# Reordering the products of an expert layer, moving the combinations of one slot, and moving two PSUM copies from ScalarE to VectorE

## Chip, cores and metric

The kernel runs on one core of one Trainium2 chip. The metric is the time of one execution in microseconds (us), measured on the device. A profiled execution gives a span that is about 1.7 us shorter than that time; spans are compared with spans, and times with times.

## The reference

The reference is an attention over 4 batches, 8 heads, 768 positions and head size 64 (causal; in five of the heads only sinks and a window are kept), followed by 8 experts over 3,072 tokens of width 512:

```python
out = 0
for e in range(8):
    h = np.maximum(x @ w1[e], 0.0)      # 3072x512 @ 512x1024
    out += P[:, e:e+1] * (h @ w2[e])    # 1024x512; P from 8 rounds of row/column scaling
```

## The kernel before

The attention, the first expert without its weights P, and the rounds that give P run first (0 to 178 us). Then come experts 1 to 7 in chunks of 512 tokens: 42 pieces of work called works. While layer 1 of one work runs, layer 2 of the work before runs too. Both multiply by Strassen's scheme in Winograd's form: seven products in place of eight, at the price of sums before and after, made by VectorE and ScalarE.

Layer 1 of a work has two halves g of seven products. Three PSUM banks (y, z, w) collect them. Some banks are read in the middle of a sum: after product 1, ScalarE copies bank y, then TensorE adds product 6 into the same bank.

```python
def step(g, k):
    if k == 1: product(g, 1, "y", first=True);            copy(g, "1", "y")     # ScalarE
    if k == 2: product(g, 2, "z", first=True, last=True); relu_sum(g, 0, 0, "z", "1")  # VectorE
    if k == 6: product(g, 6, "y");                        copy(g, "2", "y")
    if k == 5: product(g, 5, "w", first=True);            copy(g, "5", "w")
    if k == 7: product(g, 7, "y");                        relu_sum(g, 1, 1, "y", "5")
    if k == 3: product(g, 3, "w", last=True);             relu_sum(g, 0, 1, "w", "2")
    if k == 4: product(g, 4, "y", last=True);             # last read of y: a ReLU on ScalarE

for pair in (((0, 1), (0, 2)), ((0, 6), (0, 5)), ((0, 7), (0, 3)), ((1, 1), (0, 4)),
             ((1, 6), (1, 5)), ((1, 7), (1, 2)), ((1, 3), (1, 4))):
    for g, k in pair:
        step(g, k)
    yield                      # one pair of products per slot
```

A copied sum goes into a buffer R1, R2 or R5. A work has seven slots, numbered from 0 as in the code. Each slot issues one pair of layer 1's products, then perhaps combinations (sums of weights "w" or of inputs "x", on VectorE), then one product of layer 2, then perhaps a scaling of the first expert's sums ("first", on ScalarE) or a combination of h:

```python
for slot in range(7):
    go("l1", 2 if n == 0 and slot == 0 else 1)
    if slot in (1, 3):
        go("w")
        go("x", 2)             # only while e == 1
    go("l2")
    if slot in (2, 3, 5, 6):
        go("first")            # weight_first: acc = acc * Pne, 4 a work, only while e == 1
    if slot in (2, 3):
        go("h")
# ... the whole loop under
with tc.manual_schedule(engines={mybir.EngineType.DVE}):
```

The last line matters: in the expert stage only VectorE (DVE) runs in the order of the program. For TensorE and ScalarE the compiler's scheduler picks the order.

In attention the values of the first batch arrive in another layout and are put in place through PSUM, a third at a time:

```python
def place_v(g):
    for n in range(2):
        t = ...                # PSUM, two matmuls with an identity
        nc.scalar.activation(out=v_tile(0)[:, :, 2*g + n, 0:D], in_=t..., func=AF.Copy, bias=0.0, scale=1.0)
```

The softmax here doesn't subtract the row's maximum and nothing guards it: scores larger than these inputs give would overflow.

Of the kernel before, what the change touches and what calls it, by code (L numbers as in the profile page):

```python
# [13 lines left out]
AF = mybir.ActivationFunctionType  # L14
# [22 lines left out]
def kernel(  # L37
# [13 lines left out]
    nc = tc.nc  # L51
    B, H, S, D = q.shape
# [48 lines left out]
    def v_tile(b):  # L101
        if b not in vts:
            vts[b] = ap.tile([128, H, NC, DV], F16, tag="v16", name=f"v16_{b}")
            nc.vector.memset(vts[b][:, :, :, D:DV], 1.0)
        return vts[b]
# [11 lines left out]
    def place_v(g):  # L117

        for n in range(2):
            t = psA.tile([128, 512], F32, tag="mo", bufs=3, name=f"vp_{g}_{n}")  # L120
            rows = slice(64 * n, 64 * n + 64)
            for c in range(2):
                nc.tensor.matmul(
                    out=t[64 * c:64 * c + 64, :].rearrange("p (h d) -> p h d", h=H),
                    lhsT=ident16[rows, rows], rhs=vraw[g][rows, :, c, :], start=True, stop=True,
                )
            nc.scalar.activation(
                out=v_tile(0)[:, :, 2 * g + n, 0:D], in_=t.rearrange("p (h d) -> p h d", h=H),
                func=AF.Copy, bias=0.0, scale=1.0,
            )  # L130

    def load_v_heads(b, h0, h1):
        for o in range(2):
# [15 lines left out]
    def load_expert(e):  # L149
        return load_w1(e), load_w2(e)  # L150
# [15 lines left out]
    def round_first(h0):  # L166
# [9 lines left out]
        out=ret_u,  # L176
        in_=is_retrieval.bitcast(U32).unsqueeze(0).broadcast_to([128, 2 * H]),
# [209 lines left out]
    def run(g, n):  # L387
        for _ in range(n):
            if next(g, "end") == "end":
                return False  # L390
        return True

    units = [(b, g, u) for b in range(B) for g in range(3) for u in range(2)]
    with tc.manual_schedule(engines={mybir.EngineType.Pool}):
        nc.gpsimd.affine_select(
            out=ident16, in_=ident16, compare_op=ALU.is_equal, fill=0.0,
            base=0, pattern=[[-1, 128]], channel_multiplier=1,
        )
        for o in range(2):
# [3 lines left out]
                out=f4, in_=f4, compare_op=ALU.is_ge, fill=0.0,  # L403
# [4 lines left out]
                out=w4, in_=w4, compare_op=ALU.is_ge, fill=0.0,  # L408
# [118 lines left out]
    with tc.manual_schedule(engines=engines):  # L527
# [11 lines left out]
        emit_prep(*preps.pop())  # L539
        warm(2)  # L540
        place_v(0)
        soften(r0, (1,))
        sum_later(0)
# [9 lines left out]
        sum_later(1)  # L553
        r3 = scores(3)
        place_v(1)
        finish_sums(lambda: emit_prep(*preps.pop()))
        soften(r3, (0,))
# [46 lines left out]
    for it in range(8):  # L604
# [3 lines left out]
            out=Pne, in0=Pne, in1=rr.unsqueeze(2).broadcast_to([128, NB, E]), op=ALU.mult  # L608
        )
        nc.vector.tensor_reduce(  # L610
            out=bs, in_=Pne.transpose([0, 2, 1]), axis=AX.X, op=ALU.add
# [5 lines left out]
        if it == 7:  # L617
            nc.vector.tensor_scalar(
                out=rcs, in0=rcs, scalar1=float(NTOK) / E, scalar2=None, op0=ALU.mult
            )  # L620
        nc.vector.tensor_tensor(
            out=Pne, in0=Pne, in1=rcs.unsqueeze(1).broadcast_to([128, NB, E]), op=ALU.mult
# [14 lines left out]
    def weight_first(c):  # L637

        for nb in range(4 * c, 4 * c + 4):
            nc.scalar.activation(out=acc_of(nb), in_=acc_of(nb), func=AF.Copy,  # L640
                                 bias=0.0, scale=Pne[:, nb, 0:1])
            yield
# [23 lines left out]
    def combine_w(e):  # L666
        w1, w2 = expw[e]
        X = mp.tile([128, 4, 2, 512], F16, tag="S1", name=f"S1_{e}")
        yield from left(lefts1, e, [[w1[:, 2 * k:2 * k + 2, ts(i, 512)] for k in range(2)]
                                    for i in range(2)], [X[:, j] for j in range(4)])  # L670
        X = mp.tile([128, 4, 4, 256], F16, tag="T2", name=f"T2_{e}")
        yield from right(rights2, e, [[w2[:, 4 * k:4 * k + 4, ts(n, 256)] for n in range(2)]
                                      for k in range(2)], [X[:, j] for j in range(4)])

    def combine_x(c):
        X = mp.tile([128, 4, 2, 256], F16, tag=f"T1_{c}", bufs=1, name=f"T1_{c}")
        yield from right(rights1, c, [[xT[k][:, :, CH * c + 256 * n:CH * c + 256 * n + 256]
                                       for n in range(2)] for k in range(2)],
                         [X[:, j] for j in range(4)])

    def combine_h(e, c):
        h = hTs[e, c]
        X = [mp.tile([128, 2, 4, 128], F16, tag=f"S2{j}", bufs=1, name=f"S2{j}_{e}_{c}")
             for j in range(4)]
        yield from left(lefts2, (e, c), [[h[:, :, 4 * k:4 * k + 4, ts(i, 128)] for k in range(2)]
                                         for i in range(2)], X)

    def new_h(e, c):
        hTs[e, c] = mp.tile([128, 2, 8, 256], F16, tag="hT", name=f"hT_{e}_{c}")
# [16 lines left out]
    def layer1(e, c):  # L706

        new_h(e, c)
        h = hTs[e, c]
        banks, R = {}, {}  # L710

        def product(g, k, bank, first=False, last=False):
            if first:
                banks[g, bank] = psB.tile([128, 2, 256], F32, tag="l1", name=f"l1{bank}")
            for f in range(2):
                for dc in range(2):
                    nc.tensor.matmul(  # L717
                        out=banks[g, bank][:, f, :],
                        lhsT=lefts1[e][k - 1][:, dc, ts(2 * g + f, 128)],
                        rhs=rights1[c][k - 1][:, dc, :], start=(first and f == 0 and dc == 0),  # L720
                        stop=(last and f == 1 and dc == 1), skip_group_check=True,
                    )

        def copy(g, name, bank):
            R[name] = mp.tile([128, 2, 256], F32, tag=f"R{name}", bufs=1, name=f"R{name}")
            nc.scalar.activation(out=R[name], in_=banks[g, bank], func=AF.Copy, bias=0.0, scale=1.0)  # L726

        def block(g, i, n):
            return h[:, n, 4 * i + 2 * g:4 * i + 2 * g + 2, :]

        def relu_sum(g, i, n, bank, name):
            nc.vector._custom_dve(TENSOR_ADD_SAT, out=block(g, i, n), in0=banks[g, bank],
                                  in1=R[name], s0=65504.0, s1=0.0)

        def step(g, k):
            if k == 1:
                product(g, 1, "y", first=True)
                copy(g, "1", "y")
            if k == 2:
                product(g, 2, "z", first=True, last=True)  # L740
                relu_sum(g, 0, 0, "z", "1")
            if k == 6:
                product(g, 6, "y")
                copy(g, "2", "y")
            if k == 5:
                product(g, 5, "w", first=True)
                copy(g, "5", "w")
            if k == 7:
                product(g, 7, "y")
                relu_sum(g, 1, 1, "y", "5")  # L750
            if k == 3:
                product(g, 3, "w", last=True)
                relu_sum(g, 0, 1, "w", "2")
            if k == 4:
                product(g, 4, "y", last=True)
                nc.scalar.activation(out=block(g, 1, 0), in_=banks[g, "y"], func=AF.Relu,
                                     bias=0.0, scale=1.0)

        for pair in (((0, 1), (0, 2)), ((0, 6), (0, 5)), ((0, 7), (0, 3)), ((1, 1), (0, 4)),
                     ((1, 6), (1, 5)), ((1, 7), (1, 2)), ((1, 3), (1, 4))):  # L760
            for g, k in pair:
                step(g, k)
            yield
# [88 lines left out]
    def go(name, n=1):  # L852
        run(gens[name], n)

    def body(n):
        e, c = works[n]
        if c == 0 and e + 1 < E:
            expw[e + 1] = load_expert(e + 1)
        if c == 2 and e + 1 < E:
            gens["w"] = combine_w(e + 1)  # L860
        if e == 1:
            gens["first"] = weight_first(c)
            gens["x"] = combine_x((c + 1) % NCH)
        for slot in range(7):
            go("l1", 2 if n == 0 and slot == 0 else 1)
            if slot in (1, 3):
                go("w")
                go("x", 2)
            go("l2")
            if slot in (2, 3, 5, 6):  # L870
                go("first")
            if slot in (2, 3):
                go("h")
            if n == 0 and slot == 0:
                run(combine_w(1), 9)
        if n + 1 == len(works):
            gens["l2"] = layer2_last(e, c)
            return
        gens["h"] = combine_h(e, c)
        go("h", 2)  # L880
        gens["l2"] = layer2(e, c)
        gens["l1"] = layer1(*works[n + 1])

    with tc.manual_schedule(engines={mybir.EngineType.DVE}):
        for n in range(len(works)):
            body(n)
        go("l2", 9)
# [35 lines left out]
```

## Time and profile before

| | before |
|---|---|
| time, median of the first three runs | 702.01 us |
| span of the profiled run | 700.3 us |
| start to the third placement's matmuls | 31.79 us |
| from there to a fixed transpose behind the affected rounds (first matmul into tr_0_1) | 11.70 us |
| from there to the last step of the weights P | 134.16 us |
| from there to the last matmul (expert stage) | 518.25 us |
| waits of TensorE in the expert stage, above its normal spacing | 2.96 us |

The four stretches come from the start times of named matmuls in the trace. The last row adds, over the matmuls of the expert stage, what the distance between two starts exceeds 109 ns for 256 columns (216 ns for 512), where the excess is over 30 ns. The normal spacing is what the Trainium skill gives ("TensorE: Matmul & The Clock Gate", "Wait — 56ns, not 53.3ns?"): columns / 2.4 GHz + about 2.5 ns, which is an estimate of 109 ns for 256 columns; the trace agrees (median 109 ns). The wait that the profile prints in brackets is smaller than this excess, because it starts at the modelled end of the previous matmul. At 187.00 us, for instance, the list has 0.30 us and the spacing 0.46 us.

The table of stretches of the kernel before; each engine column is its busy time in 20 us, with the number of instructions (PE is TensorE, PEld its weight loads, DVE VectorE, ACT ScalarE, POOL GpSimd; PEclk is the granted TensorE clock as a share of full speed):

```profile
core 0: us, PE busy (x) PEld busy (x) DVE busy (x) ACT busy (x) POOL busy (x), PEclk, DMA share, GB/s
180.00:200.00 20.00, 19.02 (x149) 14.40 (x148) 16.22 (x33) 20.00 (x39) 1.80 (x2) 1.00 0.49 81
200.00:220.00 20.00, 19.52 (x176) 16.75 (x174) 19.32 (x40) 14.29 (x30) 3.38 (x4) 1.00 0.37 64
220.00:240.00 20.00, 19.97 (x184) 17.67 (x182) 19.28 (x39) 11.61 (x24) 5.07 (x6) 1.00 0.43 75
260.00:280.00 20.00, 20.00 (x186) 17.94 (x184) 16.76 (x32) 10.95 (x24) 5.14 (x6) 1.00 0.79 129
```

From 260 us on, TensorE has no gap. Between 180 and 240 us it executes fewer instructions, and ScalarE is first busy all the time, then VectorE nearly so. TensorE's waits in that stretch, from the list of waits of the kernel before (engine, line waited for <- releaser: total us, times, longest):

```profile
PE l1y L717 <- ACT R_3696 L726: 0.5, 1, 0.5
PE l1y L717 <- ACT R_3540 L726: 0.4, 1, 0.4
PE l1y L717 <- ACT R_3517 L726: 0.3, 1, 0.3
PE l1y L717 <- ACT R_3618 L726: 0.3, 1, 0.3
```

All four are products into bank y behind ScalarE's copy of that bank. The timeline of the kernel before shows why the copy is late (start us, us, engine, line, operation, out<-in, count, wait and releaser in brackets):

```profile
186.32 0.63 ACT L726 ACTIVATE R_3517<-l1y 128x512 f32<-128x512 f32 x1
186.80 1.98 ACT L640 ACTIVATE acc_80<-acc_80,Pne 128x512 f32<-128x512 f32 x3
187.00 0.60 PE L717 MATMUL l1y<-T_1_3466,S_1_3450 128*128 128x256 f16 x4 [0.30 <-ACT R_3517 L726]
...
188.63 0.63 ACT L726 ACTIVATE R_3540<-l1y 128x512 f32<-128x512 f32 x1
...
189.32 0.60 PE L717 MATMUL l1y<-T_1_3466,S_1_3450 128*128 128x256 f16 x4 [0.41 <-ACT R_3540 L726]
```

Product 6 starts at 187.00. Where ScalarE is free, such a copy starts about 0.7 us after its product does (in a later work, 410.30 after 409.62). Here R_3540 begins only at 188.63, 1.63 us after the product, because three scalings (L640) stand before it in ScalarE's order.

The small waits of 0.19 us look like this in the timeline of the kernel before (VectorE's lines and TensorE's, in order of time):

```profile
215.23 0.42 DVE L663 TENSOR_TENSOR T_4_3911<-xT_76 128x512 f16<-128x512 f16 x1
...
216.03 0.87 DVE L798 SCALAR_TENSOR_TENSOR acc_81<-l2w,Pne,acc_81 128x256 f32<-128x256 f32 x2
...
216.81 0.68 DVE L732 CUSTOM_DVE_ANT_0 hT_3_3872<-l1y,R_3908 128x512 f16<-128x512 f32 x1
...
216.92 0.60 PE L717 MATMUL l1y<-xT_76,w_1_2386 128*128 128x256 f16 x4
...
217.54 0.60 PE L717 MATMUL l1y<-T_3_3730,w_1_2386 128*128 128x256 f16 x4
```

The relu sum of product 7 (L732, out of bank y) ends at 217.49. Product 4, which writes that bank, starts at 217.54 instead of 217.36. VectorE was late because of the combinations of slot **1** (L663), not those of slot 3: VectorE runs in the order of the program, where this work's slot 3 comes after that relu sum, and it had worked off the work before (at 211.85 us it stood idle for 0.17 us, waiting for ScalarE). This is read from the order; no run left out slot 1's combinations.

ScalarE in the affected rounds of attention, from the timeline of the kernel before:

```profile
33.50 0.62 ACT L127 ACTIVATE v_0_245<-vp_0_653 128x512 f16<-128x512 f32 x1
33.98 0.63 ACT L127 ACTIVATE v_0_245<-vp_1_657 128x512 f16<-128x512 f32 x1
34.45 0.64 ACT L322 ACTIVATE xT_77<-xt_1_1_661 128x512 f16<-128x512 f16 x1
34.93 1.08 ACT L462 ACTIVATE PT_2_0_1_644<-sc_1_1_671 128x1024 f16<-128x1024 f32 x1
```

### The profile page before, as it was taken

The numbers are of one execution on the slowest core, as the hardware profiler recorded it, in microseconds if no ns is written. First come the engines' busy times: TensorE is split into PE (matmuls) and PEld (weight loads), VectorE is DVE, ScalarE is ACT, GpSimd is POOL, SyncE is SP. The second block draws the span as 40 slices with busy tenths as digits, with TensorE's granted clock in tenths as the row PEclk, the third lists the DMA queues.
The fourth block names the chain that finished last, engine by engine and source line by source line (L and its number), as shares of the span: only waits on it lengthen the run. The fifth ranks groups of instructions, "written<-read, shape, count | busy, mean of one in ns | idle before, by whom it ended". The sixth has DMA issues, their size and how long they took to land.

```text
span 700.3 us, 17004 instructions
## 1 busy us (share of the span) xinstructions
PE 685.8 (98%) x6913; PEld 568.5 (81%) x6913; DVE 565.3 (81%) x1147; ACT 416.5 (59%) x777; POOL 151.4 (22%) x183
## 2 busy tenths in 40 slices
PE   7999999999999999999999999999999999999997
PEld 3666666666588888888888888888888888888885
DVE  7785765757889988888898879887898888888785
ACT  6787676774886555555555555565555555555551
POOL 7431220000012131222212222122212212121210
PEclk9999999999999999999999999999999999999999
DMA  9999591000734378346934594349533964245775
GB/s 179 183 194 127 46 77 18 3 1 1 121 58 74 53 122 135 63 76 101 149 55 69 91 158 77 56 69 161 90 65 62 142 113 78 48 76 107 144 163 146
DMA packets 84255, 65.61 MB, mean 94 GB/s; under 512 B 48336, under 2 KB 64720, under 8 KB 84176
## 3 DMA queue, kind: packets, MB, share of 16 engines
q0 software_dynamic: 74976, 57.17, 57.8%
q1 hardware_dynamic: 7552, 6.30, 3.8%
q8 instruction: 54, 0.88, 0.5%
q10 hardware_dynamic: 1648, 1.05, 0.5%
q14 instruction: 25, 0.20, 0.1%
HBM read 52.45 MB, written 6.29 MB: 84 GB/s over the span
## 4 chain that ended last, share of the span: by engine, by line
PE 71%; ACT 0%; DVE 0%; issue 0%
PE l1y L717 20%; PE l2y L781 20%; PE l2w L781 10%; PE l1w L717 10%; PE l2z L781 5%; PE l1z L717 5%; PE last_10646 L833 0%; PE last_10658 L833 0%; PE last_10634 L833 0%; PE last_10682 L833 0%; PE last_10670 L833 0%; ACT R_3696 L726 0%; DVE acc_84 L838 0%; ACT add L795 0%
## 5 line engine op out<-in xcount | busy, mean ns | idle before, releaser
L795 ACT ACTIVATE add<-l2w,Pne 128x256 f32<-128x256 f32 x80 | 33.7, 473 | 65.7 <-PE l2w L781 65.7
L795 ACT ACTIVATE add<-l2y,Pne 128x256 f32<-128x256 f32 x80 | 33.8, 474 | 10.6 <-PE l2y L781 10.5
L795 ACT ACTIVATE add<-l2z,Pne 128x256 f32<-128x256 f32 x80 | 33.7, 473 | 8.7 <-PE l2z L781 8.7
L360 PEld LDWEIGHTS <-w_0_124 128*128 128x128 f16 x384 | 35.4, 98 | 4.1 <-issue 0.2
L803 POOL DMA_DIRECT2D acc_79<-add x21 | 17.7, 844 | 78.9 <-ACT add L795 60.8
L803 POOL DMA_DIRECT2D acc_81<-add x21 | 17.7, 844 | 68.9 <-ACT add L795 67.1
L803 POOL DMA_DIRECT2D acc_80<-add x21 | 17.7, 845 | 67.9 <-ACT add L795 67.9
L803 POOL DMA_DIRECT2D acc_82<-add x21 | 17.8, 847 | 67.1 <-ACT add L795 67.1
L803 POOL DMA_DIRECT2D acc_83<-add x18 | 15.1, 841 | 54.4 <-ACT add L795 47.2
L803 POOL DMA_DIRECT2D acc_84<-add x18 | 15.4, 856 | 44.3 <-ACT add L795 37.6
L798 DVE SCALAR_TENSOR_TENSOR acc_79<-l2y,Pne,acc_79 128x256 f32<-128x256 f32 x42 | 18.3, 477 | 7.2 <-PE l2y L781 7.1
L798 DVE SCALAR_TENSOR_TENSOR acc_83<-l2y,Pne,acc_83 128x256 f32<-128x256 f32 x44 | 19.2, 478 | 3.2 <-PE l2y L781 3.2
L798 DVE SCALAR_TENSOR_TENSOR acc_81<-l2y,Pne,acc_81 128x256 f32<-128x256 f32 x42 | 18.3, 477 | 4.1 <-PE l2y L781 4.1
L798 DVE SCALAR_TENSOR_TENSOR acc_82<-l2y,Pne,acc_82 128x256 f32<-128x256 f32 x42 | 18.3, 477 | 4.1 <-PE l2y L781 4.1
L798 DVE SCALAR_TENSOR_TENSOR acc_80<-l2y,Pne,acc_80 128x256 f32<-128x256 f32 x42 | 18.3, 477 | 4.1 <-PE l2y L781 4.1
L798 DVE SCALAR_TENSOR_TENSOR acc_84<-l2y,Pne,acc_84 128x256 f32<-128x256 f32 x36 | 15.7, 477 | 7.1 <-PE l2y L781 7.1
L717 PEld LDWEIGHTS <-S_4_5832 128*128 128x128 f16 x192 | 18.8, 98 | 2.2
L717 PEld LDWEIGHTS <-S_7_8934 128*128 128x128 f16 x192 | 18.8, 98 | 2.2
L717 PEld LDWEIGHTS <-S_2_3728 128*128 128x128 f16 x192 | 18.8, 98 | 2.2
L717 PEld LDWEIGHTS <-S_6_7900 128*128 128x128 f16 x192 | 18.8, 98 | 2.2
L717 PEld LDWEIGHTS <-S_5_6866 128*128 128x128 f16 x192 | 18.8, 98 | 2.2
L717 PEld LDWEIGHTS <-S_3_4798 128*128 128x128 f16 x192 | 18.8, 98 | 2.2
(2563 smaller groups left out, 2251.8 us busy)
## 6 DMA issues: line engine op xcount, KB each, us to landing
acc_79<-add POOLq DMA_DIRECT2D x21, 256.0 KB, 3.3
acc_80<-add POOLq DMA_DIRECT2D x21, 256.0 KB, 3.3
acc_81<-add POOLq DMA_DIRECT2D x21, 256.0 KB, 3.3
acc_82<-add POOLq DMA_DIRECT2D x21, 256.0 KB, 3.3
acc_83<-add POOLq DMA_DIRECT2D x18, 256.0 KB, 3.6
acc_84<-add POOLq DMA_DIRECT2D x18, 256.0 KB, 10.2
w_0_124<-in_moe_w_dram POOLq DMA_DIRECT2D x1, 1024.0 KB, 12.4
w_0_131<-in_moe_w_dram POOLq DMA_DIRECT2D x1, 1024.0 KB, 18.3
```

Of the source, the lines that this page charges most:

```text
L360: nc.tensor.matmul(out=l1[:, ts(fb % 2, 256)], lhsT=w1[:, dc, ts(fb, 128)], rhs=xT[dc // 2][:, dc % 2, c0:c0 + 256], start=(dc == 0), stop ...
L717: nc.tensor.matmul(out=banks[g, bank][:, f, :], lhsT=lefts1[e][k - 1][:, dc, ts(2 * g + f, 128)], rhs=rights1[c][k - 1][:, dc, :], start=( ...
L781: nc.tensor.matmul(out=banks[bank][q], lhsT=lefts2[e, c][k - 1][:, q, f, :], rhs=rights2[e][k - 1][:, f, :], start=(first and q == 0 and f ...
L795: nc.scalar.activation(out=t[:, q, :], in_=banks[bank][q], func=AF.Copy, bias=0.0, scale=w)
L798: nc.vector.scalar_tensor_tensor(out=dst, in0=banks[bank][q], scalar=w, in1=dst, op0=ALU.mult, op1=ALU.add,)
L803: nc.gpsimd.dma_start(out=acc[c][:, i, n, :, :], in_=t, accum_op=ALU.add)
```

## The change

The intent: leave ScalarE and VectorE more time between reading a bank and the next product into it, move combinations away from the crowded middle of a work, and give two copies in attention to an idle engine. The whole diff, but for a blank line:

```diff
-            nc.scalar.activation(
-                out=v_tile(0)[:, :, 2 * g + n, 0:D], in_=t.rearrange("p (h d) -> p h d", h=H),
-                func=AF.Copy, bias=0.0, scale=1.0,
-            )
+            dst, src = v_tile(0)[:, :, 2 * g + n, 0:D], t.rearrange("p (h d) -> p h d", h=H)
+            if g == 2:
+                nc.vector.tensor_copy(out=dst, in_=src)
+            else:
+                nc.scalar.activation(out=dst, in_=src, func=AF.Copy, bias=0.0, scale=1.0)
...
-        for pair in (((0, 1), (0, 2)), ((0, 6), (0, 5)), ((0, 7), (0, 3)), ((1, 1), (0, 4)),
-                     ((1, 6), (1, 5)), ((1, 7), (1, 2)), ((1, 3), (1, 4))):
+        for pair in (((0, 1), (0, 2)), ((0, 5), (0, 6)), ((0, 3), (1, 1)), ((0, 7), (1, 2)),
+                     ((1, 5), (1, 6)), ((0, 4), (1, 7)), ((1, 3), (1, 4))):
...
-            if slot in (1, 3):
+            if slot in (1, 5):
```

## The prediction

> **What bounds it now.** From about 178 us (expert layers) TensorE is the limit: the table of stretches has it busy 20.00 of every 20 us from 260 to 680 us. The Trainium skill ("Perfetto Trace Analysis", Identifying the Most-Contended Engine) warns that matmul busy time is a poor measure; so I use the spacing of its starts in the trace, 109 ns for 256 columns. Over the 4,592 matmuls of the two layers only about 3 us lie above 109 ns each. VectorE (16 to 18 of 20) and ScalarE (11 of 20) hide behind that.
>
> The 3 us sit in expert 1, where ScalarE also scales the first expert's sums (24 Copies, 128x512) and is busy 20.00 of 20 us from 180 to 200. Four waits make most of it: at 187.0 (0.46 us), 189.3 (0.57), 195.0 (0.44) and 201.0 (0.62), in the list of waits "l1y <- ACT R": a product into bank y waits for the copy of that bank ("PSUM - Partial Sum Buffer", Terms, forbids both at once; here the product at 187.00 starts just after the copy of 186.32 to 186.95). With small rests, 2.4 us. Three more, 0.19 us each at 217.6, 230.0 and 242.4, are product 4 of the first half behind VectorE, filled by slot 3's combinations (19.3 of 20 us).
>
> In attention ScalarE runs without a gap from 31.4 to 39 us: the placements of v's last third (0.62 and 0.63 us, starts 0.48 apart) stand at 33.50, ahead of exponentials whose scores were ready at about 33.1; VectorE is idle there for 1.6 us.
>
> **What the change does.** Nothing is added or removed: same products, copies (0.60 us), relu sums (0.68), combinations (0.42 and 0.68).
> 1. Between products 1 and 6 TensorE has 1.75 us of other work instead of 1.31 (a product of layer 1 is 0.44 us, of layer 2 0.87); from 6 to 7, 2.6 instead of 1.31; in the second half 1 to 6 goes from 1.31 to 3.05. But 5 to 3 stays at 1.31, and 6 to 7 in the second half.
> 2. Product 4 of the first half comes 3.05 us after 7, and the combinations leave slot 3: the 0.19 us waits should go. In the second half 7 to 4 tightens from 1.75 to 1.31; the relu sum is issued ahead of slot 5's combinations, so I expect no wait.
> 3. The placements move to idle VectorE, about 1 us off ScalarE's queue.
>
> **Worth.** Of the 2.4 us the longer distances take about 1: the 24 scalings still run, ScalarE stays full to about 205 us, and product 3 behind copy 5 inherits part of the wait. Plus 0.5 for the small waits, plus 0.4 of the 1 us in attention. Sum 1.9: 702.0 - 1.9 = **700.1 us**, range **698.7 to 701.8**. Chances: over 2% faster 0.01, within 2% 0.98, slower 0.01.
>
> **What would show it.** Right: waits of "l1y" behind ACT R in 185 to 202 us shrink or become waits of "l1w" (product 3); none at product 4 in 215 to 245; later works still 12.23 us; exponentials near 33.5 us start about 1 us earlier, the expert stage about 0.4 us. Wrong: a wait at product 4 or 7 of the second half in each work; "l1z" waiting for a bank.
>
> **What would make it wrong.** Past the first six rounds the order on TensorE and ScalarE is the compiler's choice; another order can cost or win a microsecond. A repeated 0.2 us wait in slots 6 or 7 would cost 8 us over 41 works. If the scalings fall differently, all 2.4 us may go.

## The result

The changed kernel took 700.85 us (median of 4 runs, 700.8 to 701.04); the kernel before, run beside it, 701.97 us (701.68 to 702.25). The ratio of the fast runs is 0.9985, with a 95% interval from 0.9967 to 1.0002. The interval includes 1, so this set alone does not show a gain. A second set (f1 below) gave 700.71 against 702.53 us, ratio 0.9973 [0.996, 0.9985].

The table of stretches of the changed kernel:

```profile
180.00:200.00 20.00, 18.66 (x150) 14.47 (x149) 16.11 (x32) 20.00 (x40) 1.80 (x2) 1.00 0.48 81
200.00:220.00 20.00, 19.76 (x180) 17.36 (x178) 19.38 (x40) 14.34 (x28) 4.00 (x5) 1.00 0.34 59
220.00:240.00 20.00, 20.00 (x186) 17.92 (x184) 19.63 (x41) 11.59 (x24) 4.44 (x6) 1.00 0.47 81
```

From 220 us on TensorE is now full (so is every later stretch up to 680 us): 186 matmul records against 184 before in 220 to 240 us. Between 180 and 200 us ScalarE is as full as before, and TensorE's matmuls rose only from 149 to 150. The list of waits of the changed kernel, in the same stretch:

```profile
PE l1w L718 <- ACT R_3541 L727: 0.8, 1, 0.8
PE l1y L718 <- ACT R_3624 L727: 0.5, 1, 0.5
PE l1w L718 <- ACT R_3720 L727: 0.2, 1, 0.2
```

Two of the four waits on l1y became waits on l1w. The timeline of the changed kernel shows one of them:

```profile
185.84 0.64 ACT L727 ACTIVATE R_3517<-l1y 128x512 f32<-128x512 f32 x1
...
186.06 0.60 PE L718 MATMUL l1w<-T_1_3466,S_1_3450 128*128 128x256 f16 x4
...
186.31 1.99 ACT L641 ACTIVATE acc_80<-acc_80,Pne 128x512 f32<-128x512 f32 x3
...
186.52 0.60 PE L718 MATMUL l1y<-T_1_3466,S_1_3450 128*128 128x256 f16 x4
...
188.15 0.64 ACT L727 ACTIVATE R_3541<-l1w 128x512 f32<-128x512 f32 x1
...
188.84 0.60 PE L718 MATMUL l1w<-xT_77,S_1_3450 128*128 128x256 f16 x4 [0.85 <-ACT R_3541 L727]
```

Product 5 (186.06) and product 6 (186.52) no longer wait. But the same three scalings stand before the copy of bank w, and product 3 waits 1.01 us by the spacing of the starts. Before, products 6 and 7 had waited 0.46 and 0.57 us at this place, which is 1.03 us together. In later works of expert 1 product 7 of the second half has hardly any slack now. In the four works between 203 and 250 us VectorE's relu sum frees R5, copy 5 of the second half starts 0.12 us after it (219.08 after 218.96), the copy of product 6 follows, and product 7 starts 0.05 us after that copy's end (220.22 after 220.17).

In attention ScalarE goes straight from the exponential at 32.74 to the copy of the transposes (xT); timeline of the changed kernel:

```profile
32.38 0.69 DVE L129 CAST v_0_245<-vp_0_653 128x512 f16<-128x512 f32 x1 [1.27 <-PE vp_1_657 L123]
...
33.45 0.68 DVE L129 CAST v_0_245<-vp_1_657 128x512 f16<-128x512 f32 x1
...
33.64 0.62 ACT L323 ACTIVATE xT_77<-xt_1_1_661 128x512 f16<-128x512 f16 x1
...
34.12 1.05 ACT L463 ACTIVATE PT_2_0_1_644<-sc_1_1_671 128x1024 f16<-128x1024 f32 x1
```

Relative to the placement's matmuls (31.79 us before, 31.94 here) the exponential on sc_1_1 starts 0.96 us earlier.

### The profile page after: what moved, and what is told of

Same layout as the page of the kernel before. It is cut to its first block, busy times and chain, and to the rows that moved or that the text cites. A ratio compares the mean times of both kernels' runs of the same rounds, so it can differ in the third digit from the quotient of the medians.

```text
span 699.1 us, 17004 instructions
## 1 busy us (share of the span) xinstructions
PE 683.9 (98%) x6913; PEld 568.7 (81%) x6913; DVE 570.9 (82%) x1149; ACT 419.8 (60%) x775; POOL 151.4 (22%) x183
## 4 chain that ended last, share of the span: by engine, by line
PE 92%; ACT 4%; DVE 2%; issue 1%; POOL 0%; ACTq 0%
PE l1y L718 20%; PE l2y L783 20%; PE l1w L718 10%; PE l2w L783 10%; PE l1z L718 5%; PE l2z L783 5%; PE l1b L698 1%; ACT acc_81 L641 0%; PE l_3312 L375 0%; PE l_3246 L375 0%; PE l_1684 L375 0%; PE l_1568 L375 0%; ACT PT_1_0_0_318 L463 0%; PE last_10658 L835 0%; PE last_10646 L835 0%
## 5 line engine op out<-in xcount | busy, mean ns | idle before, releaser
L361 PEld LDWEIGHTS <-w_0_124 128*128 128x128 f16 x384 | 35.4, 98 | 4.0 <-issue 0.2
L800 DVE SCALAR_TENSOR_TENSOR acc_83<-l2y,Pne,acc_83 128x256 f32<-128x256 f32 x44 | 19.2, 477 | 2.9 <-PE l2y L783 2.9
L800 DVE SCALAR_TENSOR_TENSOR acc_79<-l2y,Pne,acc_79 128x256 f32<-128x256 f32 x42 | 18.3, 478 | 3.1 <-PE l2y L783 3.0
L800 DVE SCALAR_TENSOR_TENSOR acc_82<-l2y,Pne,acc_82 128x256 f32<-128x256 f32 x42 | 18.3, 478 | 3.0 <-PE l2y L783 3.0
L800 DVE SCALAR_TENSOR_TENSOR acc_81<-l2y,Pne,acc_81 128x256 f32<-128x256 f32 x42 | 18.3, 477 | 3.0 <-PE l2y L783 3.0
L800 DVE SCALAR_TENSOR_TENSOR acc_80<-l2y,Pne,acc_80 128x256 f32<-128x256 f32 x42 | 18.3, 477 | 2.9 <-PE l2y L783 2.9
L718 PEld LDWEIGHTS <-S_5_6866 128*128 128x128 f16 x192 | 18.8, 98 | 2.2
L718 PEld LDWEIGHTS <-S_2_3728 128*128 128x128 f16 x192 | 18.8, 98 | 2.2
L718 PEld LDWEIGHTS <-S_6_7900 128*128 128x128 f16 x192 | 18.8, 98 | 2.2
L718 PEld LDWEIGHTS <-S_7_8934 128*128 128x128 f16 x192 | 18.8, 98 | 2.2
L718 PEld LDWEIGHTS <-S_3_4798 128*128 128x128 f16 x192 | 18.8, 98 | 2.2
L718 PEld LDWEIGHTS <-S_4_5832 128*128 128x128 f16 x192 | 18.8, 98 | 2.2
L718 PEld LDWEIGHTS <-S_1_3450 128*128 128x128 f16 x160 | 15.6, 98 | 4.1 <-issue 2.1
```

The source lines that it names most:

```text
L361: nc.tensor.matmul(out=l1[:, ts(fb % 2, 256)], lhsT=w1[:, dc, ts(fb, 128)], rhs=xT[dc // 2][:, dc % 2, c0:c0 + 256], start=(dc == 0), stop ...
L718: nc.tensor.matmul(out=banks[g, bank][:, f, :], lhsT=lefts1[e][k - 1][:, dc, ts(2 * g + f, 128)], rhs=rights1[c][k - 1][:, dc, :], start=( ...
L800: nc.vector.scalar_tensor_tensor(out=dst, in0=banks[bank][q], scalar=w, in1=dst, op0=ALU.mult, op1=ALU.add,)
```

## The experiments

Twelve runs were made, one of them (f1) the changed kernel again. All results were correct but for f4 and g4, which are wrong on purpose. Each profile is of one execution. The table gives, for each profile, the same four stretches as above, and TensorE's waits of the expert stage in its first 75 us (to about 251 us), where expert 1 runs.

| run | start to third placement | to the fixed transpose | to the last step of P | expert stage | waits to 251 us |
|---|---|---|---|---|---|
| before | 31.79 | 11.70 | 134.16 | 518.25 | 2.96 |
| after | 31.94 | 11.07 | 134.16 | 517.56 | 2.28 |
| e1_place | 32.46 | 11.07 | 134.17 | 518.53 | 2.95 |
| e2_order | 32.34 | 11.70 | 134.17 | 519.53 | 4.14 |
| e3_slots | 31.52 | 11.70 | 134.16 | 519.40 | 3.76 |
| e4_order_slots | 31.42 | 11.70 | 134.16 | 517.56 | 2.28 |
| f1_after_again | 31.82 | 11.07 | 134.18 | 517.54 | 2.27 |
| f2_after_act_order | 31.25 | 11.07 | 134.17 | 518.46 | 2.78 |
| f4_before_noscale | 31.21 | 11.70 | 134.16 | 517.03 | 0.94 |
| g1_all_order | 32.04 | 11.07 | 134.17 | 518.17 | 2.90 |
| g3_scale_early | 32.50 | 11.07 | 134.17 | 515.95 | 0.05 |
| g4_after_noscale | 31.80 | 11.07 | 134.17 | 515.27 | 0.00 |
| g5_order_two_R | 32.11 | 11.70 | 134.18 | 519.70 | 4.09 |

(f3_after_pool, with a pause of 20 us, is told below.) Three things can be read before any single run. The first stretch varies from 31.21 to 32.50 us without relation to the change; part of it follows the landing of the first inputs (the first transposes start at 7.17 to 7.74 us, late where those inputs land late), and where the rest arises was not followed. The second and third stretches repeat to 0.02 us, so the second shows the placement alone. The waits of expert 1 repeat to about 0.01 us: e4 and both runs of the changed kernel have the same five. After 251 us some profiles have one or two single waits of 0.09 to 0.86 us, at places that differ from run to run; in f4 and g3 the list of waits shows ScalarE held up by an accumulating DMA, in others the cause was not followed. They are not counted as effects of a kernel.

The theory at the outset (A) was that three separate gains add: placement, order, slots. The rivals are named with each run.

### e1_place: only the placement on VectorE

```diff
+            if g == 2: nc.vector.tensor_copy(out=dst, in_=src)     # order and slots as before
```

> Only the placement of v's last third moved to VectorE. Theory A (three separate gains that add): the expert stage starts 0.4 to 0.5 us earlier, its waits stay as before (2.4 us behind ScalarE's copies, 3 x 0.19 us at product 4): about 701.5 us, 0.5 us below before. Rival: the earlier start in the changed kernel is chance of the start of the run (DMA arrival), then within 0.1 us of before.

Measured: 702.34 us against 702.56, ratio 0.9996 [0.9983, 1.0008]. The time shows nothing, but the profile does. The affected stretch took 11.07 us instead of 11.70, a gain of 0.63 us, which is the same in every kernel with the placement and absent in every kernel without it. This run's first stretch happened to be 0.67 us longer than that of the profile of before, which hid it. The expert stage has the old waits. So the placement's gain is real, and was 0.63 us and not 0.4 to 0.5. The order of TensorE's instructions in these rounds changed as well (the compiler orders them there), so the 0.63 us is shown for the edit as a whole; that all of it is ScalarE's shorter queue is argued from the exponential's earlier start and not tested apart.

### e2_order, e3_slots, e4_order_slots: the parts of the change in the expert stage

```diff
e2: only the new list of pairs;  combinations in slots (1, 3)
e3: only "if slot in (1, 5)";     old list of pairs
e4: both;                         placement on ScalarE as before
```

> Only the order of layer 1's products; combinations still in slots 1 and 3. Theory A: the order alone takes away the 0.19 us waits at product 4 too (it now comes two slots later), and the waits behind copies go from 2.4 to about 2.3 us: in all 0.6 to 0.7 us less, about 701.3 us. Rival: the 0.19 us waits are the slots' doing, and the order alone gains 0.1 us or less.

> Only the combinations from slots 1 and 3 to 1 and 5, old order of products. Theory A: VectorE reaches the relu sum of product 7 earlier in slot 3, so the three 0.19 us waits at product 4 of the first half go; but the second half's 7 then follows the combinations of slot 5 by a slot, so waits may turn up there; the 2.4 us behind ScalarE's copies stay. 701.4 to 702 us. Rival: no change in any wait.

> Order and slots together, placement as before. Theory A (the parts add): 0.65 us below before, and 0.45 us above the changed kernel: about 701.3 us; waits in the expert stage as in the changed kernel, 2.3 us, the longest about 1.0 us at product 3 behind copy 5. Rival: without the earlier start of the stage the waits fall otherwise and the sum differs by over 0.3 us.

Measured against 702.56 us: 703.24 (ratio 1.0007 [0.9993, 1.0021]), 703.32 (1.001 [0.9997, 1.0022]) and 701.75 us (0.9984 [0.9972, 0.9997]). By the waits, each part alone makes the stage **worse**: by 1.18 us (e2) and 0.80 us (e3). Both together gain 0.68 us. Theory A, that the parts add, is false here; e4's own sum, 0.68 us, was as expected. In e2 the waits behind copies up to 209 us came to 2.29 us, as expected too: that is the order's effect on them, 0.1 us. The compiler's TensorE order in expert 1 also differs, in e2 from the changed kernel's and in e3 from that of the kernel before in more than the edit asks for, so e2 and e3 measure each edit together with that order; ScalarE's order in e2 is that of the changed kernel, in e3 that of the kernel before.

With the new order alone (e2) the combinations are still in slot 3, where in the new order the relu sums of product 7 and of the second half's product 2 stand as well. VectorE gets behind. In each of the three works from 215 to 250 us two waits follow (0.09 and 0.19 us in the work before them). The second half's product 7 waits 0.37 us, and product 3 of layer 2 waits 0.19 us for a late combination of h, although the compiler put it six matmuls later than in the changed kernel. The timeline of e2 shows the first wait beginning on ScalarE:

```profile
220.70 0.60 ACT L726 ACTIVATE R<-l1w 128x512 f32<-128x512 f32 x1 [0.37 <-DVE hT L732]
...
221.19 0.59 ACT L726 ACTIVATE R<-l1y 128x512 f32<-128x512 f32 x1
...
221.83 0.60 PE L717 MATMUL l1y<-T,S 128*128 128x256 f16 x4 [0.20 <-ACT R L726]
```

The second half's copy of bank w may not overwrite R5 until VectorE's relu sum has read the first half's R5. The next copy, and product 7 behind it, are late by as much.

With the new slots alone (e3) product 4 of the first half still comes one slot after product 7. VectorE now enters each work later, because slot 5 is near the work's end (the first combination of h starts 0.87 us after product 1, at 212.15; before, 0.16 us ahead of it), and the wait grows from 0.19 to 0.50 us, although the compiler put four matmuls of layer 2 (0.44 us) ahead of product 4; timeline of e3:

```profile
217.05 0.68 DVE L732 CUSTOM_DVE_ANT_0 hT<-l1y,R 128x512 f16<-128x512 f32 x1
...
217.78 0.60 PE L717 MATMUL l1y<-T,w 128*128 128x256 f16 x4 [0.33 <-DVE hT L732]
```

So the new order takes product 4 away from the place that slot 5 makes late, and slot 5 frees the place that the new order needs.

### g5_order_two_R: is the single buffer R5 the cause in e2?

```diff
 e2, and: R[name] = mp.tile([128, 2, 256], F32, tag=f"R{name}", bufs=1 -> bufs=2)
```

> Order alone, with two buffers for each copied sum (R) instead of one; orders of all engines as in the run with order alone. Theory: there the waits of 0.37 us at the second half's product 7 come from copy 5 of that half, which may not overwrite R5 before the relu sum of the first half's product 7 has read it; they go here, while the 0.19 us waits of layer 2 behind VectorE stay. Rival: they come from VectorE or ScalarE being late by themselves and stay.

Measured: one run, 703.76 us; the orders of all engines are those of e2. The waits of 0.37 us are gone, as expected. But the waits of 0.19 us behind VectorE became 0.55 us, so a work loses as much as before (0.55 against 0.37 + 0.19 us). The buffer decides only where the delay shows; its source is VectorE's lateness.

### f4_before_noscale, g4_after_noscale: without the 24 scalings (wrong results on purpose)

```diff
-            gens["first"] = weight_first(c)
+            pass
```

> The kernel before without the 24 scalings; its result is wrong on purpose. Theory A: the 2.4 us behind copies at 187 to 209 us vanish, the three waits of 0.19 us at product 4 stay, since VectorE causes those. Rival: the waits at 187 and 189 us stay at 0.4 us or more, because the copy after product 1 or 6 is too close to the next product whatever ScalarE's load is.

> The changed kernel without the 24 scalings; wrong result on purpose. Theory A: no wait above 0.1 us in the expert stage before 250 us. Rival: something is left at product 3 or 7.

Measured: 700.22 and 698.38 us, one run each. In the kernel before, every wait behind a copy up to 251 us vanished, and what is left are waits of 0.19 us at product 4: five of them, not three, apparently because two had been hidden under the longer waits (TensorE's order in expert 1 differs a little from before here; in g4 it is that of the changed kernel). In the changed kernel **no** wait is left in the whole expert stage, and it takes 515.27 us. With this order of products the stage has nothing left to lose in waits. Both results say that the scalings on ScalarE cause the 2.4 us before and the 2.28 us after. The distances between the products do not cause them by themselves.

### f1_after_again, f3_after_pool: the changed kernel again, and the scalings on GpSimd

```diff
 f3: -  nc.scalar.activation(out=acc_of(nb), in_=acc_of(nb), func=AF.Copy, scale=Pne[:, nb, 0:1])
     +  nc.gpsimd.tensor_scalar(out=acc_of(nb), in0=acc_of(nb), scalar1=Pne[:, nb, 0:1], op0=ALU.mult)
```

> The changed kernel once more, beside the next three on one chip. Expert stage as before: five waits, 2.28 us in all, at the same places. Time 0.8 to 1.2 us below the kernel before.

> The changed kernel, scalings on GpSimd instead of ScalarE. Theory A: the five waits behind copies vanish as in the runs without scalings, unless GpSimd slows VectorE or its accumulating DMAs come late; about 2 us below the changed kernel, less what such a new wait costs. Rival (ScalarE's load is not the cause): same as the changed kernel within 0.3 us.

Measured: f1 700.71 us, with the same five waits (2.27 us) and 1.82 us below before, which is more than expected; the nine runs of before on this chip lay between 702.14 and 703.34 us, and the waits do not explain the rest. f3 took 721.33 us, ratio 1.0266 [1.0252, 1.028]. Up to 200 us its waits behind copies shrank from 1.7 us (1.01 and 0.66) to 0.24 us, as theory A says. But one scaling takes 1.64 us on GpSimd against 0.72 to 0.85 us on ScalarE (medians), and GpSimd also issues the accumulating DMAs. From the timelines of GpSimd, ScalarE and TensorE in f3:

```profile
199.20 22.61 POOL L641 TENSOR_SCALAR acc<-acc,Pne 128x512 f32<-128x512 f32 x14
221.76 2.63 POOL L804 DMA_DIRECT2D acc<-add  x3
...
225.16 0.84 ACT L796 ACTIVATE add<-l2z,Pne 128x256 f32<-128x256 f32 x2 [22.86 <-DMA acc<-add]
...
227.03 1.01 PE L718 MATMUL l1y<-T,S 128*128 128x256 f16 x4 [20.56 <-ACT R L727]
```

The DMAs stand behind the scalings, ScalarE's three add buffers stay full, the copies come late, and TensorE stops for 20.6 us. Afterwards its matmuls of 256 columns start 213 ns apart for about 3.5 us. The Trainium skill ("TensorE: Matmul & The Clock Gate", Part 1) says that an idle array drops to half clock and needs about 3.4 us of work to return; this run agrees.

### f2_after_act_order, g1_all_order: ScalarE in the order of the program

```diff
 with tc.manual_schedule(engines={mybir.EngineType.DVE
+                                 , mybir.EngineType.Activation            # f2
+                                 , mybir.EngineType.PE                    # g1 as well
                                  }):
```

> The changed kernel, with ScalarE's order in the expert stage as the program writes it, so that the 24 scalings stand behind the copies of their slot instead of being put ahead of them by the compiler. Theory A (the 2.28 us left are copies queued behind scalings): of the five waits at most 0.5 us is left, 1.8 us or more below the changed kernel. Rival (the distance from a copy to the next product into its bank is itself too short on ScalarE): the waits stay, or come back in every work.

> The changed kernel with all three engines (ScalarE, VectorE, TensorE) in the program's order in the expert stage; TensorE's and VectorE's orders are then the same as in the changed kernel, only ScalarE's differs. Theory A: the 2.28 us behind copies fall to about 0.5 us (about 0.08 us at product 6 in each of five works, since the scaling of slot 7 still stands before copy 1), and the waits of 0.48 us that the run with ScalarE's order alone showed do not come, because they belonged to TensorE's other order. About 1.7 us below the changed kernel's expert stage. Rival: the 0.48 us waits come with ScalarE's order itself.

Measured: f2 701.39 against 702.53 us (ratio 0.9982 [0.997, 0.9995]) and g1 701.53 against 702.15 us (0.999 [0.9976, 1.0004]). Both expectations were missed. The waits at 187 to 209 us went. In their place each work of expert 1 has one wait of about 0.48 us and one of 0.08 us, 2.78 and 2.90 us in all. In f2 the list puts the longer wait down to VectorE: the compiler had placed the first matmul of layer 2's product 3 ahead of product 7, and it waits for a combination of h (done at 218.80 us; the copy that product 7 needs, at 218.81). In g1 the wait is at product 7 itself. In g1 TensorE's and VectorE's orders are exactly those of the changed kernel, so f2's explanation by TensorE's other order falls; it is ScalarE's order. The timeline of g1 (VectorE, ScalarE, then TensorE):

```profile
212.26 0.69 DVE L733 CUSTOM_DVE_ANT_0 hT<-l1z,R 128x512 f16<-128x512 f32 x1 [0.40 <-ACT R L727]
...
217.81 0.68 DVE L733 CUSTOM_DVE_ANT_0 hT<-l1y,R 128x512 f16<-128x512 f32 x1
...
218.00 0.72 ACT L641 ACTIVATE acc<-acc,Pne 128x512 f32<-128x512 f32 x1
218.62 0.59 ACT L727 ACTIVATE R<-l1w 128x512 f32<-128x512 f32 x1
219.10 0.59 ACT L727 ACTIVATE R<-l1y 128x512 f32<-128x512 f32 x1
...
219.75 0.60 PE L718 MATMUL l1y<-T,S 128*128 128x256 f16 x4 [0.32 <-ACT R L727]
```

The program itself puts a scaling in slot 3, just before the two copies of slot 4. The second half's product 7 comes 1.31 us after product 6, and a work has no slack there. But a second path ends at the same time. VectorE waited 0.40 us at 212.26 for the copy of product 1, which stood behind the scaling of the last slot; it did not catch up, and its relu sum freed R5 only at 218.49. The copy into R5 at 218.62 starts 0.13 us after that, as it does in the changed kernel without a scaling before it. In the first of the five works that wait, VectorE was not late, the copy started 0.50 us after the relu sum, and the scaling in slot 3 alone cost product 7 0.49 us (at 194.17). In the other four both paths hold the copy to the same moment, so moving the scaling of slot 3 alone would probably not have cured them; no run tried it, and g3 moves both. The scalings were at fault in both orders, but not through how many they are, as g3 shows: what counts is before which copies they stand. The 0.08 us wait is the scaling of the work's last slot (slot 6 from 0; the text on record counts it as 7), which precedes the next work's copy of product 1.

### g3_scale_early: the scalings where ScalarE is idle

```diff
 g1, and:
-            if slot in (2, 3, 5, 6):
-                go("first")
+            if slot < 3:
+                go("first", 1 + (slot == 2))
```

(The expectation counts slots from 1.)

> As the run before, with the scalings put where ScalarE is idle in the changed kernel's steady works: one at the end of slot 1, one of slot 2, two of slot 3. Theory A: nearly no wait left in the expert stage (below 0.3 us), about 2 us below the changed kernel, some 3 us below the kernel before: about 699 us. Rival (the scalings must cost TensorE something wherever they stand, as ScalarE is full): 1 us or more of waits stays.

Measured: 698.83 us (698.67 to 699.81) against 702.15 us, ratio 0.9954 [0.9942, 0.9967]. The list of expert 1's waits is empty but for 0.05 us. One single wait of 0.65 us came at 554 us, behind a late accumulating DMA, which is why the profiled stage is 515.95 and not 515.3 us. The table of stretches of g3:

```profile
180.00:200.00 20.00, 20.00 (x163) 15.66 (x162) 17.98 (x36) 16.76 (x32) 2.61 (x3) 1.00 0.56 92
200.00:220.00 20.00, 20.00 (x186) 17.94 (x184) 19.67 (x41) 14.91 (x29) 3.35 (x4) 1.00 0.35 61
220.00:240.00 20.00, 20.00 (x186) 17.92 (x184) 19.64 (x40) 16.07 (x31) 4.22 (x5) 1.00 0.42 72
```

TensorE issues 163 matmuls in 180 to 200 us, against 149 before and 150 after. ScalarE drops from 20.00 to 16.76 us in that stretch and has more to do at 220 to 240. The 24 scalings start from 180.4 to 239.5 us here, as the program spreads them over six works. In the kernel before, the compiler had pulled all of them to between 179.9 and 205 us. So the full ScalarE of 180 to 200 us was made by the order, and the rival, that the scalings must cost something wherever they stand, is refuted. This version beats the kernel before clear of noise. The changed kernel was not run beside it, but took 700.71 and 700.85 us in its own sets, and its expert stage 517.56 us against 515.95.

## Why the prediction came true, and where it did not

- **Total.** Predicted 700.1 us (698.7 to 701.8); measured 700.85 and 700.71 us. The gain of 1.1 us in the first set was put at 1.9 us. The traces account for it: the expert stage 518.25 - 517.56 = 0.69 us, the placement 11.70 - 11.07 = 0.63 us, and the first stretch 0.15 us worse by chance. The sum is 1.17 us, against 1.2 us between the two spans. The largest term of the prediction, 1 of the 1.9 us, gave only 0.11 us; that the total lay in the range all the same was luck: the range was wide, and the attention gave more than was put down for it.
- **"Of the 2.4 us the longer distances take about 1" was wrong.** This is the mis-sized term. The waits behind copies, with the small rests that the prediction counted in, fell from 2.39 to 2.28 us, by 0.11 us. The prediction had seen that product 3 would inherit part of the wait; at the first place it inherited nearly all of it (1.01 us in place of 1.03). Of the 2.28 us, 1.41 now stand at product 3, 0.75 at product 7 of the second half and 0.12 at product 6. While ScalarE has no idle time, TensorE advances only as fast as ScalarE delivers copies, and a longer distance merely chooses which product waits. f4 and g4 show the source, and g3 shows that it was the compiler's order of the scalings.
- **"ScalarE stays full to about 205 us"** was right for the changed kernel, but the reason given, "the 24 scalings still run", was not: in g3 they all run, and ScalarE is not full.
- **"Plus 0.5 for the small waits"** was right in size (0.57 us) and wrong in mechanism. The waits came from slot 1's combinations, not from those of slot 3 as the prediction had it. Neither the order nor the slots removes them at a profit: alone, they add 1.18 and 0.80 us. Only together do they gain.
- **"Plus 0.4 of the 1 us in attention"** was too low: 0.63 us, identical in all profiles.
- **The second half's product 4** does not wait, as expected. The warned-of repeated wait in the last slots did not come in the changed kernel; that there is hardly any slack at product 7 before them (0.05 us after the copy) was seen only when g1 moved the scalings.

## What to carry to other kernels

When an engine that feeds the bottleneck is shown as 100% busy in a stretch, ask first what work is in it and whether it has to be there at that time. More distance for the bottleneck only moves the wait, while spreading the filler work took all of it away. Here the compiler's scheduler had put low-priority work ahead of urgent copies as soon as it was ready, so give such work a place by hand, and check the place behind which no slack is left. Judge changes of 0.1% by fixed stretches and listed waits of the trace: two parts of a change can each lose alone and gain together, and medians with a scatter of 1 us do not show it.

## What the Trainium skill lacked or had wrong

- "GPSIMD Engine Reference", 4.1 Engine selection, says that one-input elementwise work on GpSimd is roughly at line rate. In f3 one scaling (128x512 f32, in place, one scalar per row) took 1.56 to 2.34 us, median 1.64, against 0.71 to 0.86 us for the same work on ScalarE. Fourteen in a row took 22.61 us, which confirms the single times. VectorE was at work meanwhile, and no run timed it without that, or the same work on VectorE.
- No page that we read warns that GpSimd's own arithmetic delays the DMAs issued behind it on that engine. In f3, 14 scalings in a row held three accumulating DMAs back and TensorE stopped for 20.6 us.
- "TensorE: Matmul & The Clock Gate" says that the moment of warm-up varies by about 0.5 us from run to run. No page that we read gives how much a whole kernel's start varies: in the 13 comparable profiles the same matmuls, some 32 us in, came at 31.21 to 32.50 us, although later stretches repeat to 0.02 us.
- Where the pages were right here: the rule for the spacing (109 ns measured for 256 columns), and the half clock after a long pause (213 ns measured for about 3.5 us) ("TensorE: Matmul & The Clock Gate").
